# Gated linear attention and a convolutional feed-forward: q, k and gate logits packed in three row blocks instead of four

## The chip, the cores and the metric

The kernel runs on one core of a Trainium2 chip. A core has TensorE (PE: matmuls, with its weight loads shown as PEld), VectorE (DVE), ScalarE (ACT), GpSimd (POOL) and SyncE (SP, which here issues every DMA transfer). SBUF is the on-chip memory of 128 partitions, PSUM the one that matmuls write. The metric is the device time of one execution in microseconds (us).

## The reference

Two stages, with B = 4 sequences of S = 768 steps, H = 8 heads of D = 48 features and a hidden width of 1024.

```
f = 1 / (1 + exp(-f_logit))                         # a gate per head, step and feature
for t in range(S):
    state = f[:, :, t, :, None] * state + k_t v_t^T # 48 x 48 per head
    y[:, :, t] = q_t @ state
x = y with the heads side by side                   # [B, S, 384]
h = relu(x @ w_in)                                  # 384 -> 1024
g = sigmoid(conv over 3 steps of h, per channel)
out = (h * g) @ w_out                               # 1024 -> 384
```

All inputs but the two weight matrices and the convolution's weights are float32; those three are float64, and the kernel splits each into a high and a low part itself.

## The kernel before, in words

**The attention.** The 768 steps of a sequence are cut into six chunks of 128, which makes 24 chunks. Within a chunk the decay is the running sum of log-gates, so the recurrence becomes matmuls. Features lie on partitions, time on columns. Heads come in four pairs; a pair puts one head's 48 features on partitions 0 to 47 and the other's on 64 to 111. Partitions 48 to 63 and 112 to 127 are a gap that the host fills with a copy of other features, so that a chunk's f is a tile of 128 x 512 and its k and q together one of 128 x 1024. Per chunk, in order:

- SP loads f (L381), k and q (L401) and v (L403).
- ACT makes the softplus of -f in two passes, `Exp` (L389) and `Ln` (L391); from the third group on, one pass covers three chunks.
- DVE adds up along time with a scan (L407). `runs`, a tile of ones with zeros at each pair's first column, restarts the sum.
- ACT takes the exponential of the sum (L410) and of its negative (L412). POOL copies the last column, the whole chunk's decay, into `ft_all` (L414).
- DVE multiplies k and q by the two exponentials in one instruction (L416), in place. This is called the product below.
- PE turns k round with four transposes (L422); ACT or DVE copies them to `kp` (L425).
- PE makes the scores, two heads for each of four pairs (L433); DVE masks them (L436).
- PE adds the carry, q times the state so far (L448), and the value matmuls, scores times v (L455). ACT and DVE split the result into high and low parts in `xT` (L465, L467).
- PE makes the rank update, k times v (L477). DVE adds it to the state and multiplies by the chunk's decay from `ft_all` (L484, L487, L489).

**Bringing rows together.** Chunks come in eight halves of three. In a half's `xT` the fourth pair stands in a block of its own; six transfers from SBUF to SBUF (L497) move it into the gap rows of the other three, so that the first weight matmul contracts over three full blocks of 128 rows.

**The feed-forward.** For each half, PE makes the first weight matmul (L527: 72 matmuls of 128 x 128 by 384 columns). ACT applies relu (L537) and the convolution's middle tap (L543), DVE the other two taps (L547), ACT tanh (L551), DVE the gating (L553). For each 128 steps the result is split (L570, L574), the second weight matmul follows (L583, 24 matmuls), and the output is stored (L589, L591). The weights themselves are split once at the start (L294 to L328), with PE joining the parts (L323 to L325).

**The order of the work.** All instructions are handed to a planner first. Each has an engine, an estimated duration, what it needs, which buffers it takes from which ring, and a due time from `CFG` (chunk number plus an offset for its kind). The planner simulates the five engines and writes the instructions in the order in which it would start them. On the chip every engine runs its own list strictly in that order. In the plan SP holds back an issue while eight transfers are under way. Rings: two buffers for f (three chunks each), four for k and q, four for v, two for the exponentials, one PSUM tile each for the scores and for Y.

After the planned part a count of `ft_all` decides whether a slow, exact path runs (L602 on); it doesn't here.

## Time and profile before

| what | value |
|---|---|
| timed runs | median 336.3 us (335.67, 336.3, 337.32) |
| profiled execution: its time | 336.67 us |
| profiled execution: its span | 334.9 us, 6741 instructions |
| mean granted TensorE clock | 0.996 |
| busy share of the span | PE 93%, PEld 86%, DVE 81%, ACT 69%, POOL 9% |
| DMA | 37.50 MB, mean 112 GB/s |

The span runs from the first to the last instruction; the time has some fixed work around it. A busy share is an average over stages with different limits. Matmuls are pipelined and the ends of their records are modelled, so a busy PE says that it has work, and the pitch between starts says how fast it goes. A row of a group gives line, engine, operation, output and inputs, shapes and count, then busy time and mean duration in ns, then the idle time of the engine just before and what ended it. A row of waits gives who waited for whom, the total in us, how often, and the longest. A row of the timeline begins with start and duration in us.

### The profile page before, as it was taken

Reading aid. Unit: us, or ns where it says so; the run is one execution under the profiler, and the core shown is the slowest. Engines: PE = TensorE matmul, PEld = TensorE weight load, DVE = VectorE, ACT = ScalarE, POOL = GpSimd, SP = SyncE. Lnnn points to the kernel's source line nnn. Section 1 sums busy time; section 2 is a strip of 40 time slices with the busy share of each in tenths; the row PEclk is TensorE's granted clock in tenths of the full one; section 3 lists DMA queues with packets and bytes.
Section 4 is the critical chain, followed back from the end, with each engine's and each line's share of the span. In section 5 each row is a group of like instructions: output and inputs, shape, how many; then the busy total and the mean of one; then the engine's idle time right before and its main releaser. Section 6 shows DMA issues by size and latency. Waiting matters only on the chain.

```text
span 334.9 us, 6741 instructions
## 1 busy us (share of the span) xinstructions
PE 311.0 (93%) x2707; PEld 287.0 (86%) x2707; DVE 269.8 (81%) x380; ACT 229.6 (69%) x367; POOL 31.0 (9%) x69
## 2 busy tenths in 40 slices
PE   0199999999999999999999999999999999999993
PEld 0176788889999999789889998999999999999992
DVE  6997999999999979899999852799994189587210
ACT  6868889868868897969995541875683396675320
POOL 2110100301014300010010400021000001000000
PEclk9999999999999999999999999999999999999998
DMA  6999841241034456245231014502100003001111
GB/s 218 402 398 392 324 126 32 76 125 67 0 121 131 143 164 233 94 135 180 89 91 56 25 48 135 178 33 89 24 14 2 23 32 76 25 0 47 46 42 42
DMA packets 17451, 37.50 MB, mean 112 GB/s; under 512 B 2540, under 2 KB 8708, under 8 KB 17412
## 3 DMA queue, kind: packets, MB, share of 16 engines
q1 hardware_dynamic: 17412, 37.00, 33.5%
q8 instruction: 23, 0.38, 0.5%
q14 instruction: 16, 0.13, 0.1%
HBM read 29.91 MB, written 4.72 MB: 103 GB/s over the span
## 4 chain that ended last, share of the span: by engine, by line
PE 63%; DVE 19%; ACT 10%; issue 3%; DMA 3%; SPq 1%; DVEq 0%; ACTq 0%
PE mm L583 31%; PE mm L527 18%; DVE g L547 4%; PE A L433 4%; PE Y L455 4%; DMA fb<-in_f_logit_dram 3%; PE Y L448 2%; DVE am L436 2%; DVE kq L416 2%; DVE fb L407 2%; PE ss L422 2%; DVE xT L467 1%; DVE gx L298 1%; PE Y L477 1%; DVE g L553 1%
## 5 line engine op out<-in xcount | busy, mean ns | idle before, releaser
L527 PE MATMUL mm<-xT,wi 128*128 128x384 f32 x576 | 107.4, 342 | 0.7 <-ACT hb L537 0.6
L583 PE MATMUL mm<-wo,gx 128*128 128x384 f32 x576 | 104.3, 340 | 0.1
L583 PEld LDWEIGHTS mm<-wo,gx 128*128 128x128 f32 x576 | 101.5, 188 | 0.8 <-ACT hb L537 0.4
L527 PEld LDWEIGHTS mm<-xT,wi 128*128 128x128 f32 x576 | 99.3, 188 | 3.2 <-ACT hb L537 1.8
L547 DVE SCALAR_TENSOR_TENSOR g<-hb,cw,g 128x385 f32<-128x385 f32 (+1 forms) x128 | 74.5, 616 | 6.3 <-ACT g L543 5.4
L574 DVE TENSOR_TENSOR gx<-g,gx 128x1024 fp32r<-128x1024 f32 (+2 forms) x28 | 29.8, 1070 | 22.0 <-PE mm L583 20.3
L537 ACT ACTIVATE hb<-mm 128x384 f32<-128x384 f32 x64 | 30.7, 487 | 16.8 <-PE mm L527 15.9
L543 ACT ACTIVATE g<-hb,cw 128x384 f32<-128x384 f32 (+1 forms) x64 | 38.4, 616 | 2.3 <-DVE gx L574 1.1
L433 PE MATMUL A<-kq 48*128 48x128 f32 x384 | 29.7, 297 | 10.6 <-DVE kq L416 10.5
L570 ACT CAST gx<-g 128x1024 fp32r<-128x1024 f32 (+2 forms) x28 | 25.9, 934 | 19.4 <-PE mm L583 15.9
L433 PEld LDWEIGHTS A<-kq 48*128 48x128 f32 x384 | 24.9, 199 | 15.2 <-DVE kq L416 10.9
L551 ACT ACTIVATE g<-g 128x768 f32<-128x768 f32 (+1 forms) x32 | 27.0, 846 | 14.7 <-DVE g L547 14.6
L436 DVE COPY_PREDICATED am<-mask,A 128x1024 f32<-128x1024 uint8 x24 | 31.6, 1315 | 1.4 <-PE A L433 1.4
L553 DVE SCALAR_TENSOR_TENSOR g<-g,hb 128x768 f32<-128x768 f32 (+1 forms) x32 | 30.5, 955 | 2.2 <-ACT g L551 2.2
L416 DVE TENSOR_TENSOR kq<-kq,e 128x1024 f32<-128x1024 f32 x24 | 29.2, 1222 | 2.1 <-DMA kq<-in_kq_dram 2.1
L407 DVE TENSOR_TENSOR_SCAN fb<-runs,fb 128x512 f32<-128x512 f32 x24 | 28.6, 1216 | 1.7 <-ACT fb L391 1.7
L455 PE MATMUL Y<-am,v 128*48 128x128 f32 (+1 forms) x384 | 26.3, 278 | 0.0
L414 POOL COPY ft_all<-e 128x4 f32<-128x4 f32 x24 | 17.0, 709 | 88.4 <-ACT e L412 88.4
L589 ACT COPY ob<-mm 128x384 f32<-128x384 f32 x24 | 11.4, 475 | 19.7 <-PE mm L583 16.6
L455 PEld LDWEIGHTS Y<-am,v 128*48 128x48 f32 (+1 forms) x384 | 20.5, 129 | 4.4 <-issue 4.1
L465 ACT CAST xT<-Y 112x512 fp32r<-112x512 f32 x24 | 14.0, 583 | 11.5 <-PE Y L477 8.9
L517 POOL COPY hb<-hb 128x4 f32<-128x4 f32 x16 | 11.0, 685 | 105.7 <-DVE g L553 105.7
(73 smaller groups left out, 282.5 us busy)
## 6 DMA issues: line engine op xcount, KB each, us to landing
kq<-in_kq_dram SPq DMA_DIRECT2D x24, 512.0 KB, 3.6
fb<-in_f_logit_dram SPq DMA_DIRECT2D x24, 256.0 KB, 4.7
v<-in_v_dram SPq DMA_DIRECT2D x24, 192.0 KB, 3.5
out_dram<-ob SPq DMA_DIRECT2D x24, 192.0 KB, 1.9
xT<-xT SPq DMA_DIRECT2D x48, 48.0 KB, 2.1
xT<-in_moe_w_in_dram SPq DMA_DIRECT2D x4, 512.0 KB, 9.8
xT<-in_moe_w_out_dram SPq DMA_DIRECT2D x4, 384.0 KB, 6.7
g<-in_moe_w_out_dram SPq DMA_DIRECT2D x4, 384.0 KB, 5.9
```

What stands on the lines that cost most here:

```text
L407: o = plan.op("DVE", 1240, lambda e, fv=fv: nc.vector.tensor_tensor_scan(fv(), runs, fv(), 0.0, ALU.mult, ALU.add), ka, need=[gate[n]], us ...
L416: ox = plan.op("DVE", 1222, lambda e, X=X, E=E: nc.vector.tensor_tensor(buf(X), buf(X), buf(E), ALU.mult), ka, need=[o2, ld_x], use=[X, E])
L433: nc.tensor.matmul(buf(("A", n))[:, j, p, :], buf(X)[r, 0, p, :], buf(X)[r, 1, p, :], start=True, stop=True)
L436: o = plan.op("DVE", 1320, lambda e, n=n, AM=AM: nc.vector.copy_predicated(buf(AM), mask, buf(("A", n))), (n, "sc"), need=[o], use=[("A", ...
L455: nc.tensor.matmul(out_of(Y, p, j, w), buf(V).rearrange("p h d -> p (h d)")[:, h * D:h * D + w], buf(AM)[:, j, p, :], start=c == 0 and p < ...
L527: nc.tensor.matmul(buf(ph)[:, :HS], wi[:, t, wl, f * P:(f + 1) * P], x_view(pl, u)[:, t, xl, :], start=(i == 0), stop=(i == 3 * KT - 1))
L537: nc.scalar.activation(hb[:, 2:HS + 2], buf(ph)[:, :HS], AF.Relu, scale=0.5)
L543: o = pl.op("ACT", 620, lambda e, cv=cv, hb=hb, n=n, f=f: nc.scalar.activation(cv(), hb[:, 1:n + 1], AF.Copy, scale=cw[:, 1, f:f + 1]), ke ...
L547: o = pl.op("DVE", 617, lambda e, cv=cv, hb=hb, n=n, f=f, w=w, sh=sh: nc.vector.scalar_tensor_tensor(cv(), hb[:, sh:n + sh], cw[:, w, f:f ...
L553: gates[u, fp] = pl.op("DVE", 960, lambda e, cv=cv, fp=fp, n=n: nc.vector.scalar_tensor_tensor(cv(), cv(), 1.0, h_b[:, fp:fp + 2, 1:n + 1] ...
L574: los.append(pl.op("DVE", 150 + 134 * nn * NF // 128, lambda e, hv=hv, lv=lv, src=src: nc.vector.tensor_tensor(lv(), src(), hv().bitcast(F ...
L583: nc.tensor.matmul(buf(po)[:, :DM], view(g)[:, f, :], wo[:, f, wl, :], start=(i == 0), stop=(i == 3 * NF - 1))
```

## The change

**Layout.** The host now puts the fourth head pair's features into the gap rows of the three others: gap row r of a side holds features 3r, 3r+1 and 3r+2 in blocks 0, 1 and 2. A chunk's f has three blocks of 129 columns (128 steps and a padding of 200.0), its k and q three blocks of 257 (128 of k, 128 of q and a padding of 1.0). Softplus, scan, exponentials and product run over these.

**Decay.** The gate of the padding column adds nothing to the sum, so column 129 holds the chunk's total. Its exponential times the padding of 1.0 leaves the chunk's decay in the last column of k and q. The state update reads it there, so it holds the k and q buffer until then; the copy to `ft_all` is only for the count at the end, and is due two chunks later.

**Moves.** For scores, carries and the decay the fourth pair must lie on partitions 0 to 47 and 64 to 111. Two transfers per chunk, from SBUF to SBUF, copy 16 rows x 3 blocks to 48 rows of a fourth block after the product. Scores, carries and the state update wait for both. The transposes don't, since they work on the three blocks; there are three of them, and two copies sort their result by head.

**Gathers.** With features in the order 3r + t the six transfers per half become two, of 144 KB.

**Priorities.** `CFG` has new numbers throughout, and the estimates of the changed instructions are new.

```
-           a=17.29, ft=-1.2, b=0.21, sc=-0.63, va=0.44, st=-5.04, ga=-14.63, w1=(1.34, 5.48, 6.21),
+CFG = dict(lf=3, sg=3, nf=6, groups=[3, 3, 3, 3, 3, 3, 3, 3], f=(-8.26, -13.85), gate=(3.65, -7.41), kq=0.27,
+           mv=-2.88, v=8.21, a=18.81, ft=-1.2, b=-9.91, sc=-1.29, va=0.23, st=-17.91, ga=-16.31,
+           w1=(1.08, 7.13, 13.83), w1s=(-1.83, 0.82, 5.51), cw=-18.67, w2=(10.74, 25.7),
...
+    PF, PX = P + 1, 2 * P + 1
...
+    for nm, n, shape in (("fb", 2, [P, GC, KT, PF]), ("kq", 4, [P, NP, PX]), ("v", 4, [P, H, D]), ("e", 2, [P, KT, PX]),
+                         ("kp", 2, [P, H * D])):
...
-        ox = plan.op("DVE", 1222, lambda e, X=X, E=E: nc.vector.tensor_tensor(buf(X), buf(X), buf(E), ALU.mult), ka,
-                     need=[o2, ld_x], use=[X, E])
+        ox = plan.op("DVE", 955, lambda e, X=X, E=E: nc.vector.tensor_tensor(buf(X)[:, :KT, :], buf(X)[:, :KT, :], buf(E), ALU.mult),
+                     ka, need=[o1, o2, ld_x], use=[X, E])
+        plan.op("POOL", 400, lambda e, X=X, b=b, c=c: nc.gpsimd.tensor_copy(ft_all[:, b, c, :], buf(X)[:, :KT, 2 * P]),
+                (n + 2, "a"), need=[ox], use=[X])
         pt = ("pt", n)
+        moved = [plan.op("SP", 430, lambda e, X=X, j=j: nc.sync.dma_start(
+            buf(X)[HP * j:HP * j + D, KT, :], buf(X)[HP * j + D:HP * (j + 1), :KT, :]), (n, "mv"), need=[ox],
+            use=[X], size=48) for j in range(2)]
...
-            for p in range(NP):
-                nc.tensor.transpose(bank(buf(pt))[:, p, :], buf(X)[:, 0, p, :], ident)
+            for p in range(KT):
+                nc.tensor.transpose(bank(buf(pt))[:, p, :], buf(X)[:, p, :P], ident)
...
+        okp = [plan.op(dict(ACT=410, DVE=460), 0, lambda e, f=heads_of: f(e, True), kb, need=[o], use=[pt], take=[("kp", KP)]),
+               plan.op(dict(ACT=250, DVE=260), 0, lambda e, f=heads_of: f(e, False), kb, need=[o], use=[pt, KP])]
...
-        o = plan.op("PE", 1092, score, (n, "sc"), need=[ox], use=[X], take=[("A", ("A", n))], mode="f")
+        o = plan.op("PE", 1092, score, (n, "sc"), need=[ox] + moved, use=[X], take=[("A", ("A", n))], mode="f")
...
-        oc = plan.op("PE", 590, carry, kv, need=[stated[n - 1], ox], use=[X], take=[("Y", Y)], mode="f") if c else None
+        oc = plan.op("PE", 590, carry, kv, need=[stated[n - 1], ox] + moved, use=[X], take=[("Y", Y)], mode="f") if c else None
...
+            ft = lambda X=X: buf(X)[r, :, 2 * P:].broadcast_to([HP + D, NP, D])
...
+                stated[n] = plan.op("DVE", 353, lambda e, new=new, ft=ft: nc.vector.tensor_tensor(new, new, ft(), ALU.mult),
+                                    ks, need=[o, ox] + moved, use=[X])
...
+        for j in range(2):
+            gathered[u].append(plan.op("SP", 450, lambda e, u=u, j=j: nc.sync.dma_start(
+                x_view(plan, u)[HP * j + D:HP * (j + 1), :KT, :, :].bitcast(F32), x_view(plan, u)[HP * j:HP * j + D, KT, :, :].bitcast(F32)),
```

More of the change, by code (lines that the diff above doesn't have):

```diff
@@ L405, in gla_moe_kernel @@
         ka, kb = (n, "a"), (n, "b")
-        fv = lambda fb=fb, i=i: buf(fb)[:, i].rearrange("p n t -> p (n t)")
-        o = plan.op("DVE", 1240, lambda e, fv=fv: nc.vector.tensor_tensor_scan(fv(), runs, fv(), 0.0, ALU.mult, ALU.add), ka,
-                    need=[gate[n]], use=[fb])
-        ev = lambda z, E=E: buf(E)[:, z].rearrange("p n t -> p (n t)")
-        o1 = plan.op("ACT", 622, lambda e, fv=fv, ev=ev: nc.scalar.activation(ev(0), fv(), AF.Exp), ka, need=[o], use=[fb],
-                     take=[("e", E)], mode="E")
@@ L412, in gla_moe_kernel @@
-        o2 = plan.op("ACT", 622, lambda e, fv=fv, ev=ev: nc.scalar.activation(ev(1), fv(), AF.Exp, scale=-1.0), ka,
+        fv = lambda fb=fb, i=i: buf(fb)[:, i]
+        o = plan.op("DVE", 970, lambda e, fv=fv: nc.vector.tensor_tensor_scan(
+            fv().rearrange("p n t -> p (n t)"), runs, fv().rearrange("p n t -> p (n t)"), 0.0, ALU.mult, ALU.add), ka,
+            need=[gate[n]], use=[fb])
+        o1 = plan.op("ACT", 513, lambda e, fv=fv, E=E: nc.scalar.activation(buf(E)[:, :, :P], fv()[:, :, :P], AF.Exp), ka,
+                     need=[o], use=[fb], take=[("e", E)], mode="E")
@@ L413, in gla_moe_kernel @@
+        o2 = plan.op("ACT", 516, lambda e, fv=fv, E=E: nc.scalar.activation(buf(E)[:, :, P:], fv(), AF.Exp, scale=-1.0), ka,
                      need=[o], use=[fb, E], mode="E")
[L414 to L417 removed]
+        ox = plan.op("DVE", 955, lambda e, X=X, E=E: nc.vector.tensor_tensor(buf(X)[:, :KT, :], buf(X)[:, :KT, :], buf(E), ALU.mult),
+                     ka, need=[o1, o2, ld_x], use=[X, E])
@@ L424, in gla_moe_kernel @@
-        o = plan.op("PE", 410, turn, kb, need=[ox], use=[X], take=[("s", pt)], mode="r")
-        okp = plan.op(dict(ACT=580, DVE=685), 0, lambda e, KP=KP, pt=pt: (
-            nc.scalar.copy if e == "ACT" else nc.vector.tensor_copy)(buf(KP), bank(buf(pt))), kb, need=[o], use=[pt],
-            take=[("kp", KP)])
+            for p in range(KT):
+                nc.tensor.transpose(bank(buf(pt))[:, p, :], buf(X)[:, p, :P], ident)
+        o = plan.op("PE", 310, turn, kb, need=[ox], use=[X], take=[("s", pt)], mode="r")
@@ L484, in gla_moe_kernel @@
                 stated[n] = plan.op("DVE", 354, lambda e, new=new, pk=pk, ft=ft: nc.vector.tensor_tensor(
-                    new, pk()[r], ft, ALU.mult), ks, need=[o, keep], use=[Y])
+                    new, pk()[r], ft(), ALU.mult), ks, need=[o, ox] + moved, use=[Y, X])
             else:
```

84 lines of the change are left out of this document (45 added, 39 removed).

## The prediction

> **What bounds the kernel now.** I read the busy table first, then the chain of work that ended last, then TensorE's own waits, then stretches of the span.
>
> ```profile
> PE 311.0 (93%) x2707; PEld 287.0 (86%) x2707; DVE 269.8 (81%) x380; ACT 229.6 (69%) x367; POOL 31.0 (9%) x69
> PE 63%; DVE 19%; ACT 10%; issue 3%; DMA 3%; SPq 1%; DVEq 0%; ACTq 0%
> ```
>
> The chain gives a fifth of the span to VectorE (DVE) and a tenth to ScalarE (ACT). Read literally, the change, which mostly shortens work of these two, would be worth much. The waits of TensorE (PE) say otherwise:
>
> ```profile
> PE A L433 <- DVE kq L416: 10.5, 2, 9.9
> PE mm L355 <- DVE c L305: 5.2, 1, 5.2
> PE Y L448 <- DVE xT L467: 0.7, 1, 0.7
> PE mm L527 <- ACT hb L537: 0.6, 1, 0.6
> PE mm L325 <- DVE ob L315: 0.4, 2, 0.2
> PE Y L448 <- DVE st L489: 0.3, 1, 0.3
> ```
>
> 9.9 of the first row and all of the second lie before the first score matmul. After it only 0.6 + 0.7 + 0.6 + 0.4 + 0.3 = 2.6 us of idle time remain. The stretches agree (span from:to, length, busy time and count of PE, PEld, DVE, ACT, POOL, granted clock, DMA share, GB/s):
>
> ```profile
> 15.40:24.50 9.10, 8.98 (x47) 7.00 (x48) 9.10 (x10) 6.33 (x10) 1.25 (x3) 1.00 1.04 399
> 24.50:46.90 22.40, 20.87 (x273) 15.83 (x272) 20.34 (x29) 18.04 (x30) 0.96 (x2) 1.00 0.82 294
> 46.90:329.10 282.20, 280.83 (x2389) 263.93 (x2387) 227.94 (x321) 193.41 (x309) 25.68 (x45) 1.00 0.26 79
> ```
>
> From 46.9 us to its last matmul PE is busy for 280.83 of 282.20 us. VectorE is released "just in time" by the order of work, so it appears on the chain, but PE has no hole there that a shorter VectorE could close. So the end is set by three things: when PE gets going, how much work it holds, and small holes of at most 2.6 us.
>
> **The change part by part.** *Transposes.* One of four per chunk goes, 24 of 96 (L422). The pitch between them is read from the one place where eight stand in a row, and from one where the weight matmuls follow directly:
>
> ```profile
> 136.90 1.09 PE L422 MATMUL ss<-ident,kq 128*128 128x128 f32 x8
> 46.51 0.66 PE L422 MATMUL ss<-ident,kq 128*128 128x128 f32 x4
> 46.93 3.37 PE L527 MATMUL mm<-xT,wi 128*128 128x384 f32 x18
> L422 PE MATMUL ss<-ident,kq x96: 270/273/473, 17.4 to 268.4; 128*128 128x128 f32 x96
> 216.14 0.59 PE ss L422 x4
> ```
>
> (1.09 - 0.27)/7 = 0.117 us; 0.42/4 = 0.105 us as the low bound; 0.59/4 = 0.148 as the high one, from the last row, which is the chain's. 24 x 0.117 = **-2.8 us** (-2.5 to -3.6), all of it on the path, because PE is full. Score, carry, value and rank keep their counts and shapes.
>
> *VectorE.* Scan (L407) from 512 to 387 columns, product (L416) from 1024 to 771:
>
> ```profile
> L407 DVE TENSOR_TENSOR_SCAN fb<-runs,fb 128x512 f32<-128x512 f32 x24 | 28.6, 1216 | 1.7 <-ACT fb L391 1.7
> L416 DVE TENSOR_TENSOR kq<-kq,e 128x1024 f32<-128x1024 f32 x24 | 29.2, 1222 | 2.1 <-DMA kq<-in_kq_dram 2.1
> L553 DVE SCALAR_TENSOR_TENSOR g<-g,hb 128x768 f32<-128x768 f32 (+1 forms) x32 | 30.5, 955 | 2.2 <-ACT g L551 2.2
> ```
>
> The product becomes about as long as the 768-column row, 0.26 us less. The scan saves between 125 x 1.04 ns (the slope between those two rows) = 0.13 and 125/512 x 1.216 = 0.30 us. Together 24 x 0.39 to 0.56 = 9 to 13 us of VectorE. The L553 row has operands that start one element off, so I charge nothing for the odd pitches of 129 and 257 there. PE reads of such pitches have no row; the nearest are two loads of the same width whose pitches differ:
>
> ```profile
> L455 PEld LDWEIGHTS Y<-am,v 128*48 128x48 f32 (+1 forms) x384 | 20.5, 129 | 4.4 <-issue 4.1
> L477 PEld LDWEIGHTS Y<-v,kp 128*48 128x48 f32 (+1 forms) x320 | 12.3, 131 | 0.0
> ```
>
> They say 2 ns a load either way, times 384 + 320 loads of scores and carries = 1.4 us as a bound on both sides; I take nothing.
>
> *ScalarE.*
>
> ```profile
> L389 ACT ACTIVATE fb<-fb x14: 612/633/1489, 4.0 to 157.8; 128x512 f32<-128x512 f32 x9, 128x1536 f32<-128x1536 f32 x5
> L425 ACT COPY kp<-ss x18: 572/586/597, 19.2 to 268.7; 128x512 f32<-128x512 f32 x18
> L425 DVE COPY kp<-ss x6: 665/684/692, 110.1 to 243.2; 128x512 f32<-128x512 f32 x6
> L537 ACT ACTIVATE hb<-mm 128x384 f32<-128x384 f32 x64 | 30.7, 487 | 16.8 <-PE mm L527 15.9
> ```
>
> (1489 - 612)/1024 = 0.86 ns a column. Two gate passes and two exponentials a chunk, each 125 to 128 columns shorter: 4 x 0.108 x 24 = 10 us. The copy of the turned keys is now two (288 and 96 columns). With 0.76 ns a column (584 less 487 over 128) and about 0.2 us fixed they take 0.41 + 0.27 against 0.58, so 24 x 0.1 = 2.4 us back. Net -8 us. None of these 17 to 21 us on two engines is on PE's path. What they can give is part of the 2.6 us of holes. I take **-1.0** (0 to -2.6); the cover is PE's queue of weight matmuls, and without it the whole amount would count.
>
> *The moves.* Each chunk gains two transfers of 48 KB, issued by SP after the product. All eight scores and all carries wait for both. The nearest row is the gather of before, 16 rows of 3,072 bytes and so the same size, from SBUF to SBUF too (min/median/max issue in ns, then min/median/max to landing in us, then the six of one half):
>
> ```profile
> L497 SPq DMA_DIRECT2D xT<-xT x48: 512/587/1837, 41.9 to 282.2; - x48
> DMA to landing us min/median/max: 2.0/2.1/3.8
> 41.89 3.91 SPq L497 DMA_DIRECT2D xT<-xT  x6
> ```
>
> So product to score grows by 2 x 0.59 + 2.1 = 3.3 us a chunk (3.1 to 7.5). PE's queue is in order: behind a waiting score stand weight matmuls, and ScalarE's relu and VectorE's convolution wait for those. A free stretch lets the order put a score behind one group of 18 (3.37 us in the row above), which covers 3.3 almost exactly. I charge **+0.3 us** in all (0 to +2). On SP, 48 moves x 0.59 = 28 us are added and 32 gathers x 0.59 = 19 us removed. SP waits for the product with later loads and stores queued behind. The loads have four buffers to run ahead in. The k and q buffer is released later, though: the state's decay now reads it.
>
> ```profile
> 130.02 0.66 PE L448 MATMUL Y<-kq,st 48*48 48x128 f32 x16
> 130.74 0.33 SPq L401 DMA_DIRECT2D kq<-in_kq_dram  x1
> 133.12 0.35 DVE L489 TENSOR_TENSOR st<-st,ft_all 112x192 f32<-112x192 f32 x1
> 134.08 1.23 DVE L416 TENSOR_TENSOR kq<-kq,e 128x1024 f32<-128x1024 f32 x1
> ```
>
> Today the carry at 130.0 frees it and the load lands as its product starts at 134.1. Freed by L489's end at 133.5, that load comes 2.8 us later. I count it inside the +2 bound. The GpSimd copy, now off every wait, the two gathers of 144 KB in place of six of 48 (3.91 us of issue down to some 1.2) and the smaller loads cost nothing or gain nothing on PE: W1 matmuls of older halves hide them.
>
> *The start* is the open term (the last two rows are of the DMA engines from 12 to 16 us):
>
> ```profile
> 14.09 1.22 DVE L416 TENSOR_TENSOR kq<-kq,e 128x1024 f32<-128x1024 f32 x1
> 15.36 2.08 PE L433 MATMUL A<-kq 48*128 48x128 f32 x16 [9.86 <-DVE kq L416]
> 22.37 1.91 PE L323 MATMUL mm<-gx,ident 128*128 128x512 f32 x2
> 50.14 1.04 PE L323 MATMUL mm<-gx,ident 128*128 128x512 f32 x2
> 45.42 1.16 PE L433 MATMUL A<-kq 48*128 48x128 f32 x16 [0.63 <-DVE kq L416]
> q1 hardware_dynamic: 465, 1.68, 103.0%
> v<-in_v_dram SPq DMA_DIRECT2D x3, 192.0 KB, 8.7
> ```
>
> The first product ends at 15.3; with six shorter scans, gates and itself, about 13.5. In an empty queue the score would start at 13.5 + 3.3 = 16.8. Loads issued between 12 and 16 us took 8.7 us to land, so with that queue it is 13.5 + 1.2 + 8.7 = 23.4. The new keys put the third pair of W1 loads (1.05 MB) behind, and f, k and q are smaller by 6 x 58 + 4 x 117 KB = 0.82 MB. At 1.68 MB in 4 us that is 4.5 us less queue: 18.9, or 3.5 us late. But PE's first work runs at half pace (2.08 against 1.16 us for 16 scores), and the weight joins (22.37) need no move and come some 2 us sooner with VectorE freer. If they go first, PE is at the same point by about 23 us. I take **0** (-1.5 for an empty queue, up to +8.0 for 23.4 with the joins queued behind).
>
> The Trainium skill (TensorE: Matmul & The Clock Gate, "What's actually happening") says the array starts at half clock and is released after some 3.4 us of sustained work. This trace agrees on the half pace but not on the length: the join at 22.37, 7 us after the first score, still takes 1.91 us where the one at 50.14 takes 1.04, though the stretch's row grants a clock of 1.00. By that rule a start broken by waits would add half of 3.4, an estimate of 1.7 us.
>
> Sum: -2.8 - 1.0 + 0.3 + 0 = -3.5. The profiled execution took 336.67 us, 1.8 around its span of 334.9: 333.2. It lies 0.37 above the median of 336.3, inside the runs' 335.67 to 337.32, so I say **333.0**.
>
> **The rivals.** (1) *The chain is literal.* Its lines, in shares of the span:
>
> ```profile
> by line: PE mm L583 30.7%; PE mm L527 17.5%; DVE g L547 4.2%; PE A L433 4.2%; PE Y L455 4.0%; issue 3.4%; DMA fb<-in_f_logit_dram 2.9%; PE Y L448 2.2%; DVE am L436 1.8%; DVE kq L416 1.7%; DVE fb L407 1.6%; PE ss L422 1.5%; DVE xT L467 1.5%;
> ```
>
> L416 and L407 are 3.3% or 11 us, and a quarter less of them is 2.7; with the transposes and an empty-queue start, 336.67 - 2.7 - 2.8 - 1.5 = 329.7. For it: that row. Against: PE's 2.6 us of holes. (2) *The gain is eaten.* The 3.5 us later score is paid in full once, cancelling the sum: about 336.4. For it: full DMA engines at the start; against: the joins can go ahead. (3) *Slower: moves queue behind loads.* One mechanism, at the first scores: both moves land behind 8.7 us of loads, and the scores stand ahead of the joins in PE's queue as they do now. PE starts at 23.4 rather than 15.4, 8.0 us lost less 3.5: 336.67 + 4.5 = 341; halfway between the two queues, at 21.2, it is 339. It decides once the first score starts after 15.4 + 3.5 + 1.7 = 20.6. For it: 103% of the DMA engines from 12 to 16 us; against: fewer bytes and later W1 loads.
>
> The Trainium skill (DMA: Bandwidth & Descriptors, "Queues, rings and completion order") has each engine take its descriptors in ring order, so a small transfer waits for all issued before it; the 8.7 us above agrees.
>
> (4) *It doesn't do what it says*: the counts and columns are fixed in the code and can't fail, but the new priorities let the planner place every instruction anew, and a bad place looks like rival 2 or 3; it has no chance of its own.
>
> **How the numbers follow.** Forecast 0.50 (own range 331 to 335), rival 1 0.12, rival 2 0.22, rival 3 0.16. No change means within 0.5%, what a measurement of this kernel can tell: 334.6 to 338.0. A little of the forecast lies above 334.6: faster 0.60, same 0.24, slower 0.16. The range leaves out the tail of rival 1 and most of rival 3: 329.5 to 338.5.
>
> **What would show it.** Right: 72 transposes; a product of 0.96 us; PE's idle after its first score still 1 to 3 us; moves of 2 to 4 us to landing after 45 us; the first score at 16 to 19 us with weight joins before or right behind it. Wrong: rows "PE A L433 or PE Y L448 waiting for DMA" of over 2 us in total after 45 us (the cover failed), a first score after 20.6 (rival 3), or PE's full stretch starting earlier than 46.9 with VectorE gone from the chain (rival 1).

## The result: 1.1% slower

The changed kernel takes 339.97 us (median of 4 runs, 339.84 to 340.47); the kernel before, run beside it, takes 336.12 us. The ratio is 1.0112, with a 95% interval of 1.0083 to 1.0140. The prediction was 333.0 us, with a range of 329.5 to 338.5: wrong in sign, and outside its range. The profiled execution took 339.94 us with a span of 338.2 us, 3.3 us more than the 334.9 us before.

The page of the changed kernel, its busy table and the slices of PE, clock, DMA share and GB/s:

```profile
PE 308.7 (91%) x2683; PEld 282.7 (84%) x2683; DVE 263.3 (78%) x398; ACT 216.2 (64%) x373; POOL 33.7 (10%) x73
...
PE   0269889999999999999999999999999999999993
...
PEclk9999999999999999999999999999999999999999
DMA  7989970534543021545353431133200002000111
GB/s 205 369 253 285 381 194 14 157 90 119 152 117 86 23 73 47 143 126 156 84 135 99 109 98 45 49 87 90 47 2 2 23 25 69 36 2 36 47 49 44
```

PE, VectorE and ScalarE have less to do: 2.3 us less (311.0 before), 6.5 us less and 13.4 us less. The span still grew, so the idle time of PE grew by 2.3 + 3.3 = 5.6 us. Two stretches tell where (columns as in the prediction; the kernel before has 33.26 and 248.72 us of PE in the same two):

```profile
0.00:50.00 50.00, 28.49 (x291) 20.52 (x292) 43.18 (x70) 32.32 (x60) 6.76 (x26) 1.00 0.86 281
50.00:300.00 250.00, 247.86 (x2212) 230.14 (x2211) 206.91 (x313) 170.13 (x293) 26.89 (x47) 1.00 0.29 79
```

Idle before 50 us went from 16.7 to 21.5 us (+4.8), idle from 50 to 300 us from 1.3 to 2.1 us (+0.9). So most of the loss lies in the first 50 us. The first 23 us of them, in the changed kernel and then in the kernel before:

```profile
0.00:23.00 23.00, 4.87 (x16) 3.05 (x16) 17.87 (x33) 15.92 (x31) 4.57 (x25) 1.00 0.85 279
```

```profile
0.00:23.00 23.00, 7.79 (x46) 6.55 (x47) 20.05 (x31) 17.65 (x29) 4.37 (x22) 1.00 0.89 334
```

PE's waits over the whole span name what it stood for:

```profile
PE ss L429 <- DVE kq L417: 12.9, 4, 7.1
PE mm L358 <- DVE c L308: 5.2, 1, 5.2
PE mm L541 <- DMA xT<-xT: 1.9, 2, 1.7
PE Y L464 <- DVE xT L483: 1.3, 3, 0.8
PE A L449 <- DVE am L452: 0.9, 2, 0.5
```

No row has PE wait for a move (`kq<-kq`), neither at the scores nor at the carries. A reader who looks for the cost of the moves among the waits finds none. What did change is who stands where. The timeline of PE at the start, and of the first two products on VectorE:

```profile
12.62 0.90 PE L429 MATMUL ss<-ident,kq 128*128 128x128 f32 x3 [7.12 <-DVE kq L417]
15.91 0.90 PE L429 MATMUL ss<-ident,kq 128*128 128x128 f32 x3 [2.39 <-DVE kq L417]
19.69 0.87 PE L429 MATMUL ss<-ident,kq 128*128 128x128 f32 x3 [2.88 <-DVE kq L417]
21.07 0.90 PE L429 MATMUL ss<-ident,kq 128*128 128x128 f32 x3 [0.51 <-DVE kq L417]
21.77 1.92 PE L326 MATMUL mm<-gx,ident 128*128 128x512 f32 x2
...
26.69 1.16 PE L449 MATMUL A<-kq 48*128 48x128 f32 x16
...
48.08 2.17 PE L541 MATMUL mm<-xT,wi 128*128 128x384 f32 x11 [1.66 <-DMA xT<-xT]
```

```profile
11.62 0.94 DVE L417 TENSOR_TENSOR kq<-kq,e 128x771 f32<-128x771 f32 x1
14.90 0.95 DVE L417 TENSOR_TENSOR kq<-kq,e 128x771 f32<-128x771 f32 x1
```

The first product is done at 12.6 us, 2.7 us sooner than before. Its score is placed at 26.7 us, 14.1 us behind the product; before, the score followed within 0.1 us (15.31 to 15.36). Until 21.8 us PE gets four groups of three transposes, and waits between them. The joins begin 0.6 us sooner than before (22.37), the first feed-forward matmul 1.15 us later (46.93). Over the whole kernel, each of the 24 scores starts at least 3.0 us after its product ends, the first four 14.0 to 16.6 us after. In the kernel before, five scores start 0.05 to 2.4 us after their product (the first two, the sixth, the eighth and the ninth) and the other nineteen 4.6 to 28.9 us after. So the new order gives every score room for its moves, and in the first four chunks that distance has grown by 7.0 to 14.1 us.

The sizes came out as worked out. The group of transposes before, then those of transposes, product and scan in the changed kernel, then the moves and gathers on the DMA queue (KB each, median us to landing), then the spread of the moves:

```profile
L422 PE MATMUL ss<-ident,kq 128*128 128x128 f32 x96 | 16.0, 296 | 0.0
```

```profile
L429 PE MATMUL ss<-ident,kq 128*128 128x128 f32 x72 | 13.6, 304 | 13.0 <-DVE kq L417 12.9
L417 DVE TENSOR_TENSOR kq<-kq,e 128x771 f32<-128x771 f32 x24 | 22.7, 953 | 0.3 <-DMA kq<-in_kq_dram 0.2
L410 DVE TENSOR_TENSOR_SCAN fb<-runs,fb 128x387 f32<-128x387 f32 x24 | 22.2, 950 | 1.4 <-ACT fb L394 1.3
```

```profile
kq<-kq SPq DMA_DIRECT2D x48, 48.2 KB, 2.2
xT<-xT SPq DMA_DIRECT2D x16, 144.0 KB, 3.8
```

```profile
DMA to landing us min/median/max: 2.1/2.2/6.3
```

72 transposes, a product of 0.953 us, moves of 2.2 us: nothing of the price list was far off (the 6.3 us is the first move of all, issued at 14.1 us among the first loads). The error must lie in what the list took for granted.

### The profile page after: what moved, and what is told of

It reads as the page before. It is cut to its first block, busy times and chain, and to the rows that moved or that the text cites. A ratio compares the mean times of both kernels' runs of the same rounds, so it can differ in the third digit from the quotient of the medians.

```text
span 338.2 us, 6775 instructions
## 1 busy us (share of the span) xinstructions
PE 308.7 (91%) x2683; PEld 282.7 (84%) x2683; DVE 263.3 (78%) x398; ACT 216.2 (64%) x373; POOL 33.7 (10%) x73
## 4 chain that ended last, share of the span: by engine, by line
PE 71%; DMA 11%; ACT 8%; DVE 5%; SPq 2%; issue 1%; ACTq 0%; DVEq 0%
PE mm L597 30%; PE mm L541 24%; PE Y L471 5%; PE A L449 4%; DMA xT<-xT 4%; DMA g<-in_moe_w_out_dram 3%; DMA kq<-in_kq_dram 3%; PE Y L464 2%; PE ss L429 2%; DMA fb<-in_f_logit_dram 2%; PE Y L493 1%; PE mm L326 1%; ACT hb L551 1%; DVE g L561 1%; DVE kq L417 1%
## 5 line engine op out<-in xcount | busy, mean ns | idle before, releaser
L597 PE MATMUL mm<-wo,gx 128*128 128x384 f32 x576 | 105.8, 340 | 0.4 <-ACT hb L551 0.3
L567 DVE SCALAR_TENSOR_TENSOR g<-g,hb 128x768 f32<-128x768 f32 (+1 forms) x32 | 30.5, 955 | 4.1 <-ACT g L565 3.9
L419 POOL COPY ft_all<-kq 128x3 f32<-128x3 f32 x24 | 19.3, 809 | 103.9 <-DVE kq L417 103.9
L449 PE MATMUL A<-kq 48*128 48x128 f32 x384 | 27.9, 285 | 0.9 <-DVE am L452 0.9
L449 PEld LDWEIGHTS A<-kq 48*128 48x128 f32 x384 | 23.3, 187 | 5.9 <-issue 3.6
L429 PE MATMUL ss<-ident,kq 128*128 128x128 f32 x72 | 13.6, 304 | 13.0 <-DVE kq L417 12.9
L603 ACT COPY ob<-mm 128x384 f32<-128x384 f32 x24 | 11.4, 477 | 19.6 <-PE mm L597 16.6
L410 DVE TENSOR_TENSOR_SCAN fb<-runs,fb 128x387 f32<-128x387 f32 x24 | 22.2, 950 | 1.4 <-ACT fb L394 1.3
L417 DVE TENSOR_TENSOR kq<-kq,e 128x771 f32<-128x771 f32 x24 | 22.7, 953 | 0.3 <-DMA kq<-in_kq_dram 0.2
```

Source lines behind the costliest of these rows:

```text
L417: ox = plan.op("DVE", 955, lambda e, X=X, E=E: nc.vector.tensor_tensor(buf(X)[:, :KT, :], buf(X)[:, :KT, :], buf(E), ALU.mult), ka, need=[ ...
L449: nc.tensor.matmul(buf(("A", n))[:, j, p, :], buf(X)[r, p, :P], buf(X)[r, p, P:2 * P], start=True, stop=True)
L567: gates[u, fp] = pl.op("DVE", 960, lambda e, cv=cv, fp=fp, n=n: nc.vector.scalar_tensor_tensor(cv(), cv(), 1.0, h_b[:, fp:fp + 2, 1:n + 1] ...
L597: nc.tensor.matmul(buf(po)[:, :DM], view(g)[:, f, :], wo[:, f, wl, :], start=(i == 0), stop=(i == 3 * NF - 1))
```

## The experiments

Eighteen kernels were run. They began with three theories. S: the moves in SP's queue delay the start. C: PE's half pace at the start sets it. O: the planner placed the instructions anew, and the new places lose the time. From e5 on there is a fourth, M: the layout itself costs. Later ones are named where they come up.

### The moves taken out of the given order (e1, e2)

e1 keeps the order of the changed kernel and issues no moves; e2 issues them into tiles that nobody reads, so that nobody waits.

```
e1_nomove
-        moved = [plan.op("SP", 430, lambda e, X=X, j=j: nc.sync.dma_start(
-            buf(X)[HP * j:HP * j + D, KT, :], buf(X)[HP * j + D:HP * (j + 1), :KT, :]), (n, "mv"), need=[ox],
+        moved = [plan.op("SP", 430, lambda e: None, (n, "mv"), need=[ox],
-                    ... buf(X)[r, p, :P], buf(X)[r, p, P:2 * P], ...
+                    ... buf(X)[r, min(p, 2), :P], buf(X)[r, min(p, 2), P:2 * P], ...
e2_spare
+            spare[n % 4][HP * j:HP * j + D, :], buf(X)[HP * j + D:HP * (j + 1), :KT, :]), (n, "mv"), need=[ox],
```

> The changed kernel with the order of every instruction kept, but the two moves per chunk not issued; scores and carries of the fourth pair read the third block instead, and the decay of the fourth pair is 1.0 (this part of the result is left out). Theory S (SP's queue: the moves hold SP and the loads behind them, and the data comes late): the 3.8 us of the change come from the moves, so 335 to 337 us, the w_in pair issued at 27.5 now before 24, and the first feed-forward matmul before 46.5. Theory C (TensorE's half pace at the start, broken by waits): little changes, 339 to 340, since the first joins still come at 21.8 at half pace. Theory O (the new order itself is bad whatever the moves do): 339 to 340.5.

> The changed kernel with the order kept and the moves issued at their places, but into spare tiles; scores and carries of the fourth pair read the third block (that part of the result is left out), so nobody waits for a move. It splits the run without moves. If SP's queue is the cost (its waits for the product and 0.6 us an issue, with loads behind), this is as slow as the changed kernel, 339 to 340. If late data is the cost, as fast as the run without moves, 335 to 337. Theories C and O: 339 to 340.5.

Measured: e1 339.94 us, ratio 1.0107 (1.0059 to 1.0156); e2 337.76 us, 1.0055 (1.0035 to 1.0074). PE's waits in e1:

```profile
PE ss L428 <- DVE kq L417: 13.1, 4, 7.4
PE mm L358 <- DVE c L308: 5.2, 1, 5.2
PE mm L540 <- DMA xT<-xT: 2.2, 2, 1.7
```

They are nearly those of the changed kernel. With the moves gone and the order kept, nothing comes back: theory S falls. That says only that the moves aren't waited for in this order. It doesn't say that they are free, since the order was written around them; that is asked below. e2 lies 2.2 us under e1, between what the theories gave; its half pace at the start ends at 24 us where that of the changed kernel ends at 26, and why wasn't followed up.

### Half pace at the start (e3, e4, e7, e8)

At the start PE needs 0.90 us for three transposes where it later needs 0.55, and 1.92 us for the pair of join matmuls where it needs 1.04 to 1.13. Idle matmuls ahead of the first real work bring PE to full pace sooner, in the changed kernel (e3, e7) and in the kernel before (e4, e8). They compute nothing that is used.

```
e3_warm, in the transposes (e7_warm_short: 8, 3, 4)
+            for _ in range((20, 6, 7)[n] if n < 3 else 0):
+                nc.tensor.matmul(buf(pt)[:, :KT * PF], ident, runs, start=True, stop=True)
e4_before_warm, in the scores (e8_before_warm_short: 10)
+            for _ in range(21 if n == 0 else 0):
+                nc.tensor.matmul(buf(("A", n))[:, 0, :, :], ident, runs.rearrange("p (n t) -> p n t", t=P), start=True, stop=True)
```

> The changed kernel with idle-time matmuls ahead of the transposes of the first three chunks (20, 6 and 7 products of the identity with the tile of ones, 387 columns, overwritten by the transposes), so that TensorE works from about 3 us on. Theory C: the joins at 21.8 run at full pace (a group of three in 1.4 instead of 2.5 us), some 2 to 4 us gained: 336 to 338. Theories S and O: TensorE only waits longer, 339.5 to 341.

> The kernel before with 21 such products of 512 columns ahead of its first score, from about 3 to 15 us. Theory C: up to 4 us gained (9 us at half pace hold 4.8 us of work), 332 to 334.5. Otherwise the first feed-forward matmul is set by VectorE and DMA, and the time stays at 336 to 337.

Measured: 348.02 us (ratio 1.0375, 1.0326 to 1.0424) and 343.68 us (1.0218, 1.0187 to 1.0248). The idle matmuls took longer than I had given them. In the kernel before (e4) they took 20.2 us instead of 12, ran to 25.5 us, and the first score came 10.2 us late:

```profile
5.42 20.18 PE L431 MATMUL A<-runs,ident 128*128 128x512 f32 x42
25.53 1.16 PE L435 MATMUL A<-kq 48*128 48x128 f32 x16
```

So these two don't tell what half pace costs, but something of lateness: 10.2 us of late score cost 7.5 us, although the scores and joins then ran at full pace. The two shorter ones ask the first question again.

> The changed kernel with 8, 3 and 4 idle-time products ahead of the transposes of chunks 0, 1 and 2, sized by the pace of the earlier run (0.69 us each at full pace, 2.6 us at half pace first), so that they end about when the products of k and q do. Theory C: first joins at 21.8 at full pace, 1.4 us for three instead of 2.5: 2 to 3 us gained, 337 to 338. Without C: 339.5 to 340.5.

> The kernel before with 10 idle-time products of 512 columns ahead of its first score, ending near 15 us by the same pace. Theory C: 16 scores in 1.1 instead of 2.1 us and joins at full pace from 22.4, 1 to 2.5 us gained: 333.8 to 335.3. Without C: 336 to 337.

Measured: 339.54 us (1.0080, 1.0043 to 1.0116) and 337.42 us (1.0022, 0.9988 to 1.0056). Both run the joins at full pace at 22 us. In their profiles the first feed-forward matmul comes 0.9 and 1.0 us sooner (47.18 after 48.08, 45.92 after 46.93), but the medians show no gain of the 1 to 3 us that theory C had: e7 can't be told from the changed kernel, e8 not from the kernel before. Theory C falls as the cause of the loss; a gain of under 1 us is too small to be seen here.

### Other orders (e5, e6, e9 to e12)

In e5 the planner got figures from the traces (loads at 0.2 MB per us in the first 6.5 us and 0.38 after, PE at half pace for the first 24 us, 1.7 us more for a gather to land, 0.62 us for a move's issue), and the due times were searched again. e6 is the same treatment of the old layout. e9 and e10 are two more sets of due times of the changed layout, e11 one more of the old.

```
e5_replan, e6_before_replan
-                    pipe = max(o.end + 1500, pipe) + o.size / 0.34
-                    seen = pipe + 700
+                    pipe = max(o.end + 1500, pipe)
+                    pipe += o.size / (0.2 if pipe < 6500 else 0.38)
+                    seen = pipe + (2400 if o.size == 144 else 700)
+                    ns *= 2 if COLD and now < COLD else 1
-CFG = dict(lf=3, sg=3, nf=6, groups=[3, 3, 3, 3, 3, 3, 3, 3], f=(-8.26, -13.85), gate=(3.65, -7.41), kq=0.27,
-           mv=-2.88, v=8.21, ...
+           f=(-6.74, -12.68), gate=(-8.82, 2.26), kq=-2.53, mv=-5.15,
+           v=27.73, ...
```

e6 has due times of its own; e9 to e11 differ in these numbers alone (v is 5.19 in e9, 8.67 in e10).

> The changed kernel, every instruction kept, but with another order: the planner's figures for the machine are set to what the traces show (transfers at 0.2 MB/us for the first 6.5 us and 0.38 after, a move's issue 0.62 us and a gather's 0.64 with 1.7 more to land, TensorE at half pace for its first 24 us), and the priorities are chosen anew for these. Theory O (the order, made for a faster start than the chip gives, is the cost): the 3.4 us lost by 45 us and the 2.5 us of extra waits after it come back, 332 to 335 us, below the kernel before by the 2.5 to 2.8 us of transposes. Theory M (the layout itself costs, by whatever it moves): 338 to 341.

> The kernel before with the same figures in the planner and priorities chosen anew in the same way. It holds the layout of before, so it tells what a new order alone is worth. Theory O, with the order of before near its best (2.6 us of waits after the first score): 334.5 to 337. If this gains as much as the changed kernel does by the same treatment (6 us, 330 to 332), the layout is worth nothing.

> Changed layout, new due times as in e5_replan, but with the due time of the v loads held early (it was 27.73 there, 8.21 in the changed kernel), because in e5_replan TensorE waited 2.0 us for a v load at 30.5 us and ran at half pace from 32.5 to about 41. Theory O (the new order of the instructions lost the time, not the layout): no wait for a v load above 0.7 us before 45 us, no second stretch at half pace, first feed-forward matmul by 46.5 us, time 333 to 335.5 us, 1 to 3 us under the kernel before. Theory M (the layout itself costs, by moves, larger gathers and the dense rows): 337 us or more however the due times stand. If the wait is gone and the time still is 336 to 338, what remains lies after 45 us, and the waits there say where.

> Changed layout with a third set of due times, found independently of the other two. It shows how far the time goes up and down with the order alone: theory O expects 333 to 339 us and a spread among the three orders (e5_replan 337.6) of more than 1 us with the same instructions; theory M expects all three within 1 us of the changed kernel's 340.

> Layout of the kernel before with a second set of due times, found in the same way as those of e9_replan_v: the control. Theory O expects 336 to 339 us, 2 to 4 us above e9_replan_v, about the 2.8 us that the transposes save. If it comes out below e9_replan_v, the layout is no gain on the chip, whatever the order.

The ratios are to runs of the kernel before beside each, whose medians were 336.07 to 336.72 us.

| order | us (median, runs) | ratio to before (95%) |
|---|---|---|
| old layout, as given | 336.12 (4) | 1 |
| old layout, e11 | 336.97 (12) | 1.0017 (0.9992 to 1.0041) |
| old layout, e6 | 338.5 (9) | 1.0058 (1.0035 to 1.0081) |
| new layout, as given | 339.97 (4) | 1.0112 (1.0083 to 1.0140) |
| new layout, e5 | 337.59 (10) | 1.0025 (0.9995 to 1.0056) |
| new layout, e10 | 339.09 (6) | 1.0108 (1.0079 to 1.0138) |
| new layout, e9 | 340.36 (6) | 1.0138 (1.0105 to 1.0171) |

After e5 and e6 alone I took theory O for supported. e9 to e11 took that back: e9 was to give 333 to 335.5 us and gave 340.4. The order moves the time by some 2.5 us in either layout. No order of the new layout gets under the old one as given; the best, e5, can't be told from it.

e5's profile also showed a stretch of half pace, from a wait of 2.0 us for the second chunk's v; PE's timeline, then the stretch from 24 to 50 us with the granted clock as its third figure from the end:

```profile
32.49 1.98 PE L475 MATMUL Y<-am,v 128*48 128x128 f32 x16 [2.00 <-DMA v<-in_v_dram]
...
35.22 2.08 PE L453 MATMUL A<-kq 48*128 48x128 f32 x16
37.23 2.07 PE L331 MATMUL mm<-gx,ident 128*128 128x512 f32 x2
```

```profile
24.00:50.00 26.00, 23.31 (x263) 17.74 (x262) 20.57 (x31) 12.01 (x25) 0.19 (x1) 0.80 0.86 293
```

e12 keeps e5's order and issues three v loads sooner.

```
+        for n, i in ((1, 9), (2, 6), (3, 6)) if self.tuned else ():
+            v = next(o for o in done if o.at == (n, "v"))
+            done.remove(v)
+            done.insert(next(k for k, o in enumerate(done) if o.at == (i, "f", int(i == 9))), v)
```

> The order of e5_replan, instruction for instruction, but for three DMA issues: the loads of the v rows of the second, third and fourth unit are issued by SyncE some 10, 4 and 4 us earlier (in e5_replan the second was issued at 25.5 us, behind six logit loads and four weight loads, and landed at 32.5 us). New due times moved everything at once in e9 and e10, so they could not tell this wait from the rest. If the 2.0 us wait at 30.5 us is what put TensorE back to half pace until 41 us: no wait for v above 0.5 us before 45 us, a granted clock above 0.95 in 24 to 50 us where it was 0.80, and 4 to 5 us less than e5_replan's 337.6: 332.5 to 334.5 us, under the kernel before by 2 to 3.5 us; the layout then isn't what costs. If the clock in 24 to 50 us stays at 0.8 to 0.9, or the time is 336 to 338 us, half pace there has another cause and the layout stays unfavourable in every order tried. The other side: the three earlier loads push the logit loads back by half a microsecond each and give 338 us or more.

Measured: 337.95 us, ratio 1.0055 (1.0020 to 1.0089). In the profiled execution, 336.61 us long, the wait is gone and the clock from 24 to 50 us is granted in full, 2.6 us less span than e5's. But e5's profile is of one of its slower runs (339.38 of 336.0 to 339.4), and e12's runs lie in two groups, 335.7 to 337.3 and 338.6 to 340.9, as a whole no faster than e5's. There are new waits, 1.9 us for a move at 43 us among them. One late load is repaired and others come late. That the start has no slack fits this, but isn't shown by it.

### The old order held (e13 to e15)

This is the comparison that the prediction had priced: the new layout, everything else in its place. Each engine executes the instructions of the kernel before in their old order, on the old engine and in the old buffers.

```
e13_old_order (in e14 and e15 too)
+AT = (...)
+ON = '...'
+            for o, t, e in zip(self.ops, AT, ON):
+                o.key, o.engs = (t, o.key[1]), {ENG[int(e)]: o.engs[ENG[int(e)]]}
...
+                    if self.tuned and o is not up[e]:
+                        continue
e14_old_order_no_moves
-        moved = [plan.op("SP", 430, ...) for j in range(2)]
+        moved = []
e15_old_order_moves_unread
-        o = plan.op("PE", 1092, score, (n, "sc"), need=[ox] + moved, ...
+        o = plan.op("PE", 1092, score, (n, "sc"), need=[ox], ...
```

`AT` holds the start of each instruction in the plan of the kernel before, `ON` its engine; `up` is the next in an engine's list. In e14 and e15 the fourth pair reads the third block, so its part of the result is left out; e15 issues the moves into tiles that nobody reads.

> The changed layout with the order of the kernel before held: on each engine the instructions stand as there, on the same engine and in the same buffers; the second copy of the turned k stands right behind the first, the two gathers where the last two of six stood, the two moves of a chunk on SyncE where the product ends. This is what the prediction priced: its moves term (+0.3, 0 to +2) took for granted that scores and carries find cover for 3.3 us more between product and score. Theory W (the latency of the moves has no cover in the old order, and the order made anew is the price paid for it): TensorE waits for moves, product to score 3 to 8 us longer in most of 24 chunks, 345 to 365 us. Theory O (nothing but the new placement lost the time): 333 to 335 us. Theory M (dense rows, larger gathers or the split copies cost by themselves): 336 to 341 us with few waits on moves.

> As e13_old_order, but with no moves at all: the fourth pair reads the rows of the third, the carried decay of the fourth is one, so the outputs of the fourth pair differ. Leaves out two transfers a chunk and every wait for them. Theory W and theory O: what is left of the change is the saved 24 transposes and the shorter vector work, 332.5 to 334.5 us, 2 to 3.5 us under the kernel before. Theory M: 336 us or more, and the waits of TensorE name the place.

> As e14_old_order_no_moves, but the moves are issued at their place on SyncE, into rows that nobody reads (the fourth pair again reads the rows of the third). It tells the wait for a move from what its issue does to SyncE's queue and to the other transfers. Theory W: within 1.5 us of e14, so the wait is the price. If SyncE's queue is the price (48 issues of 0.6 us, each behind a product, loads and stores behind them): 2 us or more above e14, with TensorE or VectorE waiting for loads of q and k, v or logits.

Measured: e13 364.14 us (ratio 1.084, 1.0783 to 1.0897), e14 350.27 us (1.0407, 1.0353 to 1.0461), e15 352.4 us (1.047, 1.0424 to 1.0516). Theories W (no cover for the moves in the old order) and O had e14 at 332.5 to 334.5 us; only M, with 336 or more, allows it, and none named its cause. The moves cost 13.9 us when waited for (e13 less e14) and 2.1 us when only issued (e15 less e14, a little over the 1.5 that W allowed), so of their price the wait is most. Yet 14 us remain without any move. The waits of e14, of all engines and of SP's queue:

```profile
DVE kq L507 <- DMA kq<-in_kq_dram: 13.9, 7, 3.2
PE mm L628 <- DMA xT<-xT: 6.8, 3, 4.4
```

```profile
SPq L494 <- DVE st L592: 78.1, 12, 14.0
SPq L494 <- DVE st L587: 32.2, 4, 14.5
```

and the same two of the kernel before:

```profile
DVE kq L416 <- DMA kq<-in_kq_dram: 2.1, 2, 1.2
```

```profile
SPq L401 <- PE Y L448: 49.9, 11, 11.2
```

Before, SP waited with a chunk's k and q load (L401) for the carry, PE's last reader of the buffer. Now (L494) it waits for the state update on VectorE, which reads the decay from the padded column of that buffer. The load comes late, the product waits for it, and what stands behind the load in SP's queue is late too.

### The padded column and the moves, one at a time (e16, e17)

e16 is e14 with one edit more: the state update reads the decay from GpSimd's copy, as the kernel before did. e17 is e16 with the moves done; it computes everything.

```
-            ft = lambda X=X: buf(X)[r, :, 2 * P:].broadcast_to([HP + D, NP, D])
+            ft = lambda b=b, c=c: ft_all[r, b, c, :].rearrange("p (n o) -> p n o", o=1).broadcast_to([HP + D, NP, D])
-                    new, pk()[r], ft(), ALU.mult), ks, need=[o, ox] + moved, use=[Y, X])
+                    new, pk()[r], ft(), ALU.mult), ks, need=[o, keep], use=[Y])
```

> As e14_old_order_no_moves (the order of the kernel before, no moves; the fourth pair reads the rows of the third and its carried decay is one), with one edit more: the state update takes the decay from the copy that GpSimd makes of the padded column, and no longer from the padded column itself, so that a chunk's k and q buffer is free after its carry as in the kernel before, and not only after its state update. Theory K (the padded column holds the buffer through the state update; in e14 SyncE then stands 78 us before the k and q loads for the state update L592 and the product waits 13.9 us for these loads): those waits go, time 330 to 334 us, 2 to 6 us under the kernel before, which is then also what the saved transposes and the shorter vector work are worth when nothing else is in the way. Theory G (gathers of 144 KB, which land 3.8 us after their issue): the 6.8 us of waits for gathers stay and the time stays above 342.

> As e16_no_moves_decay_copied, with the moves done and the fourth pair reading what they bring, all outputs computed: the changed layout in the order of the kernel before, with the decay copied by GpSimd after the moves. Against e16 it tells the price of the moves in an order that has no cover for them. Theory W: e16 plus the 13.9 us that e13 lay above e14, 344 to 348 us, with TensorE waiting 8 us or more for moves. If it comes out at 333 to 336, the moves cost nothing in themselves and the padded column alone forced the new order.

Measured: e16 **330.36 us**, ratio 0.9822 (0.9798 to 0.9845); e17 345.85 us, 1.0267 (1.0242 to 1.0292). Both as theories K (the padded column holds the buffer) and W had it. e16 leaves out the fourth pair's part of the result as e14 does. In e16 the wait of the product, that of SP's queue, and the group of its transposes:

```profile
DVE kq L507 <- DMA kq<-in_kq_dram: 1.2, 2, 1.0
```

```profile
SPq L494 <- PE Y L551: 54.8, 13, 11.2
```

```profile
L516 PE MATMUL ss<-ident,kq 128*128 128x128 f32 x72 | 13.0, 298 | 0.0
```

One edit took 19.9 us away. The gather waits of e14 went with it, though the gathers are the same 144 KB: they were late because a load ahead of them in SP's queue waited. Theory G (the larger gathers) falls. What is left, 6.1 us under the kernel before, is what the dense rows are worth in this order with neither cost.

e17 differs from e16 by the moves and by the waits for them. PE's waits, the stretch from 50 to 110 us (granted clock third from the end), and the first scores:

```profile
PE A L542 <- DMA kq<-kq: 8.2, 4, 5.9
PE mm L634 <- DMA xT<-xT: 2.1, 2, 1.2
```

```profile
50.00:110.00 60.00, 56.25 (x390) 50.62 (x389) 54.07 (x83) 44.14 (x76) 4.22 (x11) 0.94 0.25 67
```

```profile
15.01 1.65 PE L542 MATMUL A<-kq 48*128 48x128 f32 x12 [9.52 <-DVE kq L510]
22.61 0.98 PE L542 MATMUL A<-kq 48*128 48x128 f32 x4 [5.95 <-DMA kq<-kq]
```

Twelve of the first chunk's sixteen scores run at once, the fourth pair's four stand 6 us for the move, and with them all that is behind in PE's queue. In all the moves add 15.5 us to the median and 17.7 to the profiled span (of e17's slowest run, 347.45): 5.5 us of idle PE before 50 us, 5.4 us of it from 50 to 300 us, and 6.9 us more of busy time for the same matmuls (304.9 to 311.8), with a granted clock of 0.94 from 50 to 110 us where e16 had 1.00.

This isn't a price paid in every chunk. The 8.2 us of waits lie in three of the 24: the first (6.0), the sixth (1.2) and the eighth (1.0), all of them among the five whose scores stood close behind their products in the kernel before. The two moves of the first chunk, issued at 15.2 us among the first loads, took 7.0 us to land instead of 2.2; theory W had the wait in most chunks. The waits also cost more than their length. After the sixth chunk's wait, and one of 0.9 us for a gather, 18 weight matmuls took 6.10 us (the last row is e16's for the same ones):

```profile
kq<-kq SPq DMA_DIRECT2D x2, 48.2 KB, 7.0
```

```profile
52.62 1.12 PE L542 MATMUL A<-kq 48*128 48x128 f32 x4 [1.24 <-DMA kq<-kq]
...
55.13 6.10 PE L634 MATMUL mm<-xT,wi 128*128 128x384 f32 x18 [0.92 <-DMA xT<-xT]
```

```profile
45.05 3.37 PE L628 MATMUL mm<-xT,wi 128*128 128x384 f32 x18
```

### Decay copied, order made anew (e18)

> The whole changed computation with the decay copied (as e17_moves_decay_copied), the instructions placed anew from the order of the kernel before, chunk by chunk, so that products and moves come earlier and scores later where that shortens the whole. It asks whether cover for the moves can be had once the k and q buffer is free after the carry. If the hold of the buffer was the larger price in a fitted order: 331 to 334.5 us, under the kernel before by 2 to 5. If the cover for the moves is what costs (products some 5 us earlier fill the buffers and push loads and vector work together in the first 50 us): 335 to 339 us, as the other fitted orders.

The edit is that of e17 with other start times in `AT`: products and moves earlier, scores later, where a search over the planner's simulation, with e5's figures, found it shorter. Measured: 340.28 us (337.1 to 342.1), ratio 1.0099 (1.0059 to 1.0139), above both of the ranges that I had given. In this order the buffer is free after the carry, and the time is no better than that of the orders which hold it longer. It points to the cover for the moves as what still costs, but it is one order, with waits of its own (2.1 us for a v load, 1.8 us for a gather), and another might do better. No version that computes everything beats the kernel before.

## Why the prediction was wrong

The idle time of PE before 50 us and from 50 to 300 us, its busy time and the span, each from one profile:

| kernel | idle 0 to 50 | idle 50 to 300 | PE busy | span |
|---|---|---|---|---|
| before | 16.7 | 1.3 | 311.0 | 334.9 |
| after | 21.5 | 2.1 | 308.7 | 338.2 |
| e13 old order, moves, column | 23.9 | 14.0 | 317.4 | 361.4 |
| e14 old order, no moves, column | 19.3 | 10.8 | 311.5 | 348.7 |
| e17 old order, moves, copy | 21.8 | 6.2 | 311.8 | 345.7 |
| e16 old order, no moves, copy | 16.2 | 0.8 | 304.9 | 328.0 |

- **What bounds the kernel: right.** PE is full, and what counts is when it gets going, what it holds and its holes. e16, with all else out of the way, shows the transposes as 16.0 to 13.0 us of busy time.
- **Transposes, -2.8: right** (3.0 in e16; in the changed kernel 2.4, as it runs twelve of them at half pace at the start).
- **VectorE and ScalarE, -1.0 as holes: about right in e16, lost in the changed kernel.** e16 gains 6.9 us of span, of which 3.0 are transposes. Its first joins come 1.05 us sooner (21.32 against 22.37), and PE's idle falls by 0.8 us in all. The rest is shorter rows: 0.6 us in the joins and 2.4 in the two weight matmuls (107.4 to 106.9 and 104.3 to 102.4). Why these rows are shorter no run here shows.
- **The start, 0: this step failed in the changed kernel itself.** "If they go first, PE is at the same point by about 23 us." The joins did go first (21.8 us), but by 23 us PE had been busy 4.9 us where the kernel before had 7.8: the scores of the first two chunks were still to come. By 50 us its idle time had grown by 4.8 us, more than the 3.5 us that the whole sum was to gain. The upper bound of 8.0 us covers that size, but for another reason (joins queued behind a late score).
- **The moves, +0.3 (0 to +2): this step failed.** "A free stretch lets the order put a score behind one group of 18 ... which covers 3.3 almost exactly" took cover for granted in every chunk. In the old order nineteen of the 24 chunks had it, with 4.6 us or more between product and score; five had 2.4 us or less, and three of these made PE wait in e17. The moves cost 13.9 us (e13 less e14) or 15.5 us (e17 less e16) all the same, as the first of them took 7.0 us to land, not 3.3, and PE worked more slowly after the holes. In the changed kernel the cover is there for all, and its price stands in the start. That the first 50 us, where transfers take 86% of the DMA engines, leave no room to have products sooner is my reading of where the idle time lies; e18 is in line with it, and doesn't prove it.
- **The buffer released 2.8 us later, inside the +2: this step failed too.** The size for one load was near (in e14 seven products wait for their load, 3.2 us at most), but it was not multiplied. The buffer of every chunk is held, SP stands with the next load and with everything behind it, and in the old order this costs 19.9 us (e14 less e16). "The loads have four buffers to run ahead in" was the cover named; in the kernel before, SP already waited 49.9 us for one of these four to come free.
- **Rival 4 given "no chance of its own": the failure behind all three.** The prediction added its terms onto the old order, and treated the new one as something that could only go wrong by accident. The old order with both terms takes 364 us, so another one was needed. That one won back 24 of the 34 us that separate e13 from e16, and kept 9.6 (339.97 less 330.36). Beside e16 the changed kernel has 5.3 us more idle before 50 us, 1.3 us more from there to 300 us, and 3.8 us more of busy time; the first score stands 14 us behind its product, and no wait for a move shows. How much of the 9.6 us any order must pay, and how much a better search would find, stays open: a new search of the old layout came out 0.6% above it (e6), and the best of the new layout, e5, at 337.59 us.
- **Rival 3's sign came, its mechanism didn't, or not there.** The first score is at 26.7, past 20.6, with a time of 340 as there. But the joins stand ahead of it, not behind, and e1 without any moves takes the same time: the late score is a place in the order, not a queue of loads. In the old order of e17, where the scores do stand ahead of the joins, its mechanism is seen: the last of the first chunk's scores start at 22.6 us (rival 3 had 23.4, or 21.2 halfway), and the joins 6.4 us later than in e16 (27.70 against 21.32).
- **The signs.** Waits of PE for DMA at scores or carries, over 2 us in total after 45 us, were to show that the cover failed. There is no such row, and the moves had their price none the less: once the order has been made anew, a latency is seen in where instructions stand, and not in waits.

## What to carry to other kernels

Where a planner writes the order, an edit that lengthens a dependence or holds a buffer longer is to be priced in the old order first, for every repetition: the trace before has the distance of each from what it will wait for, and the few short ones count, most of all at the start. What a new order can win back is a guess until it is run. Taking the cause out of the finished new order (e1) says little about its price, because the order keeps the price; take it out of the old order instead. And when a small operand is tucked into a big buffer to save a copy, ask who then frees the buffer, and which loads stand behind it in the queue.

## What the runs showed that I had not expected

In some profiles PE fell back to half pace after short waits in the middle of its work. After 2.0 us (e5, at 30.5) the 16 scores again took 2.08 us, and after 2.38 us (e9) 16 value matmuls took 1.98 us. After waits of 1.66 us (changed kernel, at 46.4) and 1.85 us (e12, at 43.2) the pace stayed. e9, PE's timeline:

```profile
39.52 1.13 PE L468 MATMUL Y<-kq,st 48*48 48x128 f32 x16 [2.38 <-DVE st L509]
40.58 1.98 PE L475 MATMUL Y<-am,v 128*48 128x128 f32 x16
```

The Trainium skill (TensorE: Matmul & The Clock Gate, "What's actually happening") has the clock fall to half after an idle window of about 3.4 us. Here a wait of 2.0 us was enough in e5, so the measurement decides for this kernel. In e17 two waits of 1.24 and 0.92 us within 5 us were enough (the 18 matmuls above), so the length of one wait alone doesn't decide. The half pace lasted from 32.5 to about 41 us in e5, with a granted clock of 0.80 over 24 to 50 us. Each of these is one profiled execution.

How soon full pace came differed with the work. The idle matmuls of 128 x 128 by 512 columns, on end from 5.4 us, went from one every 0.85 us to one every 0.43 us after some 4 us in e4 and some 6 us in e8. In the kernel before, scores and transposes follow each other from 15.4 us, and the join at 22.4 us, 7 us later, still took 1.91 us; the one at 24.9 us took 1.19. Whether the kind of matmul is the reason no run here shows.

The first loads were slow in both kernels: in the first slice of 8.5 us the DMA engines of the changed kernel moved 205 GB/s with 0.7 of their time busy, in the second 369 with 0.9 (218 and 402 GB/s in the kernel before).
